# Loading a in blocks and turning it on VectorE and GpSimd instead of TensorE, in a fused RWKV-7 and gated-cosine kernel

## The chip, the cores and the metric

The kernel runs on one core of one Trainium2 chip. The metric is device time in microseconds of one execution, as the median of several runs. TensorE is called PE in the profile (its weight loads PEld), VectorE DVE, ScalarE ACT, GpSimd POOL, and SyncE, which issues most transfers, SP.

## What is computed

Two blocks follow each other: a recurrent attention (RWKV-7) over 768 steps for 4 batches x 8 heads with head size 40, and then a feed-forward layer on its output, 3072 tokens x 320 features, with 2048 hidden features.

```python
for t in range(S):
    kt, vt, rt = (k[:, :, t], v[:, :, t], r[:, :, t])
    wt, at, bt = (w[:, :, t], a[:, :, t], b[:, :, t])
    y[:, :, t] = np.einsum('bhd,bhde->bhe', rt, state)
    Sa = np.einsum('bhde,bhe->bhd', state, at)
    state_decay = state * wt[:, :, None, :] - np.einsum('bhd,bhe->bhde', Sa, bt)
    state = state_decay + np.einsum('bhd,bhe->bhde', vt, kt)
...
h = x @ w_in          # x is y, as tokens x (heads * head size)
g = h * np.cos(h)
return g @ w_out
```

All data is float32 on the chip; the two weight matrices arrive as float64 words and are rounded to float32 by the kernel itself (the items `t`, `e`, `m`, `p` of the order, each written `c`).

## The kernel before

**Units.** The sequence is cut into chunks of 64 steps (C). A unit is one chunk of two batches: its 128 partitions are 2 batches x 64 steps, its free dimension 8 heads x 40 features, padded to 64 (DP). There are 24 units (NU), handled in pairs (u, u+1) at the start of their work and one by one after that. Units of the same parity carry the same two batches.

**Within a chunk** the recurrence becomes matrix products. W is the running product of w over the steps of the chunk. The matrices need the feature dimension on the partitions (64 partitions for each of two heads, four pairs of heads `j` side by side, and in each the two batches' 64 steps: a tile of [128, 4, 128]). The steps of a unit, by their names in the order:

- `Lw La Lb Lk Lv Lr`: the loads (`load`, L128 to L149). A unit's a is loaded by two transfers of 64 steps x 8 heads x 40 features, one for each batch, in rows of 160 bytes.
- `pw` (`p1_w`): four PE transposes of w for each unit. For units 0 to 3 a scan on DVE makes the running products; from unit 4 on w arrives from memory as running products already (made for four chunks at a time on the tile `ws` by `scan`, `wj`, `sd`, stored by `ws`), and ACT copies them out of PSUM into `wb`; POOL takes the last column (`wc`) and puts a one in front (`from_one`).
- `pa` (`p1_a`): a, turned and multiplied by W. From unit 4 on: two PSUM banks, four PE transposes into each (`turned`, L370), and one product on DVE for each unit, out of PSUM into `aT` (`a_W`, L422).
- `rw` (DVE, reciprocal of W, then b times it on POOL), `pb` (b turned on PE), `pn` (the 64 x 64 products of a and b, copied by ACT), `K` (k over W on POOL, and v beside it), `v`, `k` (turned), `g` (products of k with a and v with r).
- `inv` and its steps `i`: for four units at a time a triangular inverse on DVE, 32 x 32 blocks in each of 128 partitions, with block transposes on DVE (L539, L555, L564; L617 for the first four units); `H`, `R` and `F`, `S` put the blocks together on PE.
- `t`, `q`, `ag`, `xa`, `s`, `z`: the chain from unit to unit, which hands on the state (`qz`), and at its end the result `yt`, multiplied by W on POOL (L840, 128 x 512, as the new product of the change).
- `T`, `X`: the result goes to memory and comes back as the tokens' transposed input `xT` of the second block (units 0 and 1 go straight, `Y`).

**The second block** is cut into 12 groups of tokens (two units each) x 4 parts of the hidden features, and each of these into four pieces on PE, written `M`: two of the first matmul (`ph`, L75), and two of the second (`po`, L75), which belong to the part before. Between them stand the steps `r`: rounding and cosine on ACT and DVE (L922 to L933); in the last groups (G0 on) the second matmul uses seven products in place of eight, for which DVE and POOL form sums (L981 to L989) and POOL sums of the weights (`B`, L965 to L969). `o` stores a result from SP.

**Order.** Nothing is reordered by a scheduler: `tc.manual_schedule()` keeps the instructions of each engine in the order in which they are issued, and that order is the long string `PLAN`, written out by a search. A name in it issues the whole step on all its engines and queues. A `^` makes the next PSUM tile begin with one matmul of the identity, 128 x 256, whose result is overwritten: padding on PE (`busy`, L348). A name that begins with L or f and ends with `a` issues its transfers from ACT's queue, all others from SP's. Each engine and each queue works strictly in order, so a step that waits holds up whatever stands behind it there; SP has no notion of the pieces and runs ahead of PE until something makes it wait.

The tiles into which a is loaded are two, one for each parity (`nat_a0` and `nat_a1`; units 2 and 3 use a part of w_in's place), so the load of unit u waits until unit u - 2 has been read out of its tile. PSUM has a pool of four banks (`at`) for nearly all steps of the first block, two for `ph` and two for `po`.

Of the kernel before, what the change touches and what calls it, by code (L numbers as in the profile page):

```python
# [20 lines left out]
def kernel(  # L21
# [12 lines left out]
    nc = tc.nc  # L34
# [93 lines left out]
    def load(u, names, via=nc.sync, parts=range(NB)):  # L128
        t0 = C * (u // 2)
        for n in names:  # L130
            if n == "r" and u < 4:
                x = r[NB * (u % 2) : NB * (u % 2) + NB, :, t0 : t0 + C, :].rearrange("b h t d -> (b h) (t d)")
                to = pick(nat[n, u], 0, (1, C * H * D * NB // P))
                via.dma_start(to, x.rearrange("h (g n) -> h g n", g=P // H // NB))
                continue
            for i in parts:
                at_u = src[n][NB * (u % 2) + i, :, t0 : t0 + C, :]
                if n == "w" and u >= 4:
                    at_u = wd[u // 4][NB * (u % 2) + i].rearrange("h s t d -> h (s t) d")
                    at_u = at_u[:, t0 % P : t0 % P + C]  # L140
                to = nat[n, u][blk[i], :, :D]
                if n in "vr":
                    for f in range(2):
                        via.dma_start(
                            pick(nat[n, u][blk[i]], f * DP, (2 * DP, HH), (1, D)),
                            at_u[f * HH : (f + 1) * HH].rearrange("h t d -> t h d"),
                        )
                else:
                    via.dma_start(to, at_u.rearrange("h t d -> t h d"))  # L149
# [1084 lines left out]
    with tc.manual_schedule():  # L1234
# [51 lines left out]
        def inv_begin(q):  # L1286
# [13 lines left out]
            ^ z0 c z1 ^ ^ v2 Y0 Lw4 La4 c Lw5 c Lk2 K2 Y1 La5 rw4 c ^ S3 f8 M Lk3 c f13 f9a M c c c f10 rw5  # L1300
            k2 K3 r S2 Lk4 c r c r ^ ^ t2 c c r g2 r H1 c c r ^ ^ pw4 k3 c f11 Lw7 M c f12 c c M c c ag2 r r
            Lb7 c q2 Lr3 c c wf2 c M r c c xa2 r f14 R1 pa4 c r c Lb6 M pb4 c f15 r c scan2 s2 c c pn4 La6 M
            Lw6 c c z2 lo4 ^ M v3 rw6 c c f16 c r La7 ^ g3 c wj2 t3 ^ pw6 f17 T2 ag3 c c rw7 q3 c r r c c c
            M r xa3 f18 ^ pa6 c c c M c s3 Lr4 pb6 f19 r r sd2 z3 c c M M c c pn6 M X2 lo6 r Lv4 inv1 r T3
            Lb8 X3 r c c i i i i t4 r r i i ws2 i r i M ^ v4 K4 Lk5 k4 i ^ M i g4 Lv5 i i M r i i r Lr5 r i
            M r r i i K5 r i ^ ^ ag4 i i i q4 o i i i M M M v5 r Lw9 i Lw8 r r La9 xa4 r i i r M M La8 i i i
            i pw8 i r M i wf3 t5 k5 i inv2 pa8 g5 M Lr7 H2 r Lv6 r Lb9 rw8 r r Lv7 M Lb10 H3 R2 r M ag5
            scan3 r Lk6 rw9 q5 Lr6 xa5 s4 wj3 M Lb11 s5 z4 M pb8 r Lw10 Lw11 v6 o T4 r K6 z5 La10 r r pw10 M
            rw10 La11 k6 T5 v7 rw11 R3 X4 pn8 Lk7 X5 Lr9 pa10 M r lo8 r sd3 K7 pb10 g6 pn10 Lr8 Lk8 k7 ws3 i
            i i M i lo10 M r g7 i i t6 t7 Lv9 r La13 r i i r M Lb12 i M r ag6 i i i r q6 i M i ag7 xa6 M i i  # L1310
            q7 wf4 Lw13 M r r r r o Lb13 i i Lv8 s6 r i i xa7 M r z6 T6 s7 Lw12 M t8 i i i K8 M z7 r v8 i
            Lk9 M i k8 pw12 r g8 i r r o v9 M ag8 r q8 i r rw12 K9 i M xa8 T7 Lr10 M X6 Lb14 k9 M rw13 r i
            t9 i i Lv10 i i i r La12 X7 r pb12 g9 M inv3 scan4 H4 Lk10 H5 Lw15 v10 pa12 r wj4 Lw14 r La14 R4
            Lb15 pn12 lo12 r M sd4 s8 M r r r z8 Lr11 M r ag9 q9 K10 M rw15 o t10 La15 r T8 rw14 k10 xa9
            pw14 Lb16 Lv11 pb14 r g10 s9 M pa14 z9 pn14 o M R5 ws4 r M M i lo14 Lk11 i r Lv12 r r r Lw16 r i
            i Lw17 v11 ag10 Lr12 K11 La16 Lv13 Lk12 i M T9 q10 M k11 i i i r t11 i X8 M r i r i X9 r xa10
            g11 s10 M r r i i rw16 ag11 q11 i i M M r xa11 r i z10 La17 r s11 r M M r Lr13 v12 i K12 r T10 i
            i Lb17 t12 i k12 pw16 pa16 M rw17 X10 i Lr14 M Lk13 r r r r La19 g12 M M r r v13 i M M i i i i i
            i i i r z11 ag12 r M M r r r i Lv14 r q12 M M i i i H6 r T11 r H7 M Lw19 r r La18 M K13 r R6
            Lk14 R7 xa12 r M v14 k13 s12 X11 M r pb16 r Lb19 wf5 z12 r Lw18 r pn16 K14 Lb18 r M scan5 o Lv15  # L1320
            M lo16 t13 k14 o g13 r pw18 rw18 M Lb20 M rw19 ag13 q13 r r T12 M pa18 xa13 r r r pb18 Lk15 wj5
            inv4 X12 r M s13 M Lr15 sd5 M pn18 r r r lo18 z13 M i r i M o K15 v15 r La21 k15 r t15 i Lr16 i
            i Lv16 t14 g15 T13 g14 M ag14 q14 Lk16 M r r r X13 r i i i i M r r M xa14 ag15 M q15 M r i i
            Lr17 Lv17 o r r xa15 r r i r i M ws5 M Lw20 i i s15 s14 i M Lw21 i z15 z14 M r r rw20 r r r M M
            pw20 r v16 K16 i i Lk17 i M M T14 i o r r K17 i r v17 i r M M k17 i r La20 i i r i i M Lb21 t17
            t16 k16 T15 i i pa20 Lb22 g17 Lw22 M i r Lk18 r i r r o g16 X14 M M r i r Lv18 La23 ag16 rw21
            q16 M Lr19 M i X15 r xa16 r r Lb23 r H8 H9 pb20 M R8 r R9 M s16 r M z16 M r K18 ag17 Lw23 rw23 r
            q17 r rw22 Lr18 r La22 r M M Lv19 r xa17 pw22 pa22 k18 T16 o pb22 pn20 lo20 s17 M M v19 r r v18
            r M r r r M g18 inv5 X16 z17 Lk19 pn22 i lo22 T17 i i i M M o r K19 k19 M r r r r r M g19 M M
            t18 i i Lr21 i i X17 r i r r t19 Lv20 i i M Lr20 r r i Lv21 i i B1 M i ag18 i B0 r q18 M i i  # L1330
            ag19 xa18 M i r i r i r s18 r r M r i M i i q19 r r o r M xa19 z18 Lk20 K20 s19 M r r r r B3 T18
            i z19 Lk21 v21 B2 K21 r M r r i M B6 k20 r v20 r M M r g20 r r r X18 r k21 r o M r M t20 r r t21
            T19 M ag20 B7 q20 B5 M Lk22 r i B4 r i r g21 xa20 r r M X19 M i i ag21 r r q21 i r r i i M M i r
            r xa21 Lv22 M r r H10 r H11 M r r R10 Lr23 r R11 r M Lr22 s21 s20 M o r z20 r Lv23 K22 T20 X20 r
            r r r r o r z21 r M M M M v23 Lk23 v22 r r r M r T21 M t23 K23 X21 t22 r r r r k22 k23 r M g22
            g23 M ag22 q22 M r r M r r r r r r r M M r r r xa22 M M r r r r ag23 q23 r r M M xa23 r r r M r
            r r M s23 r o r r s22 M M r z22 T22 r z23 r r M r r M r r r M M M M T23 r r r r r r r r r X22
            X23 M M r r r r r o r r M M r r M M r r r ^ M r r o M r r r r M M r M r r r o r r M r r r M M M
            M r r r r r r r r M r M o o
# [75 lines left out]
```

## Time and profile before

| what | value |
|---|---|
| median of 3 runs | 758.38 us (757.45 to 758.88) |
| the profiled execution | 761.06 us, its span 759.1 us |
| granted TensorE clock | 0.994 of full speed |
| PE | 739.2 us busy, 97% |
| DVE | 549.9 us, 72% |
| ACT | 400.4 us, 53% |
| POOL | 228.9 us, 30% |
| chain that ended last | PE 82%, DVE 7%, ACT 4%, DMA 3% |
| SP's queue (q1) | 170,104 packets, 30.4% of 16 engines' span |

How to read it: the span runs from the first to the last instruction. A row of a group gives line, engine, operation and the tiles written and read, then how many there were and how long they took; a row in order of time begins with its start and its length in us, and may end with the idle time before it and what ended that. A float32 matmul appears as two instructions, a transpose as one; the length of a PE row contains latency that overlaps the next one's, so what PE is held by is the distance from one start to the next. SPq and ACTq are transfers being issued, not moved.

### The profile page before, as it was taken

The numbers are of one execution on the slowest core, as the hardware profiler recorded it, in microseconds if no ns is written. First come the engines' busy times: TensorE is split into PE (matmuls) and PEld (weight loads), VectorE is DVE, ScalarE is ACT, GpSimd is POOL, SyncE is SP. The second block draws the span as 40 slices with busy tenths as digits, with TensorE's granted clock in tenths as the row PEclk, the third lists the DMA queues.
The fourth block names the chain that finished last, engine by engine and source line by source line (L and its number), as shares of the span: only waits on it lengthen the run. The fifth ranks groups of instructions, "written<-read, shape, count | busy, mean of one in ns | idle before, by whom it ended". The sixth has DMA issues, their size and how long they took to land.

```text
span 759.1 us, 28518 instructions
## 1 busy us (share of the span) xinstructions
PE 739.2 (97%) x12360; PEld 604.4 (80%) x12360; DVE 549.9 (72%) x1133; ACT 400.4 (53%) x778; POOL 228.9 (30%) x400
## 2 busy tenths in 40 slices
PE   7999989999999999999999999999999999999997
PEld 6877867777887887888787877787877988898886
DVE  6798979999679896579737658755379885656554
ACT  1335577655576457545475644555654536444442
POOL 5304745501420343102213103123221744312111
PEclk9999999999999999999999999999999999999999
DMA  9463665344345224533133320541021311200100
GB/s 140 116 181 81 163 149 134 100 89 87 72 111 107 65 38 88 110 67 63 29 82 67 78 73 2 105 75 37 12 57 20 77 18 21 57 7 9 44 19 18
DMA packets 177796, 54.39 MB, mean 72 GB/s; under 512 B 152712, under 2 KB 173320, under 8 KB 177672
## 3 DMA queue, kind: packets, MB, share of 16 engines
q1 hardware_dynamic: 170104, 49.17, 30.4%
q10 hardware_dynamic: 7568, 3.41, 2.0%
q8 instruction: 97, 1.59, 0.9%
q14 instruction: 27, 0.22, 0.1%
HBM read 41.68 MB, written 10.81 MB: 69 GB/s over the span
## 4 chain that ended last, share of the span: by engine, by line
PE 82%; DVE 7%; ACT 4%; DMA 3%; issue 2%; SPq 1%; POOL 0%; ACTq 0%; DVEq 0%; POOLq 0%
PE ph L75 26%; PE po L75 23%; PE x0ps L75 5%; PE dps L75 4%; PE beside L75 3%; PE gram L75 3%; PE sps L75 3%; PE vT L370 2%; PE nps L75 2%; PE below L75 1%; PE qps L75 1%; PE aps L370 1%; PE wT L370 1%; PE seventh L75 1%; PE kT L370 1%
## 5 line engine op out<-in xcount | busy, mean ns | idle before, releaser
L75 PE MATMUL ph<-xT,w_in_sb 128*128 128x256 f32 x768 | 182.7, 386 | 1.0 <-DVE gT L933 0.7
L75 PEld LDWEIGHTS ph<-xT,w_in_sb 128*128 128x128 f32 x768 | 140.4, 190 | 28.8 <-issue 9.8
L75 PE MATMUL po<-w_out_sb,gT 128*128 128x320 f32 x512 | 147.9, 438 | 0.0
L922 ACT ACTIVATE turns<-ph,rnd 128x512 f32<-128x512 f32 x96 | 62.7, 685 | 146.2 <-PE ph L75 143.8
L75 PEld LDWEIGHTS po<-w_out_sb,gT 128*128 128x128 f32 x512 | 93.9, 190 | 35.8 <-issue 0.3
L926 DVE SCALAR_TENSOR_TENSOR turns<-turns,ph 128x512 f32<-128x512 f32 x96 | 63.9, 682 | 69.1 <-ACT turns L922 65.7
L933 DVE TENSOR_TENSOR gT<-ph,turns 128x512 f32<-128x512 f32 x96 | 64.9, 682 | 25.5 <-ACT turns L930 25.0
L825 POOL TENSOR_TENSOR qz<-qz,wc 128x160 f32<-128x160 f32 x44 | 20.8, 478 | 174.4 <-DVE qz L824 172.7
L930 ACT ACTIVATE turns<-turns,half_pi 128x512 f32<-128x512 f32 x96 | 69.3, 722 | 3.1
L929 ACT ACTIVATE turns<-turns 128x512 f32<-128x512 f32 x96 | 60.3, 628 | 10.0 <-DVE turns L926 9.8
L551 DVE TENSOR_TENSOR inv<-inv,inv_tmp 128x31 f32<-128x31 f32 (+15 forms) x155 | 59.9, 387 | 5.3
L547 DVE TENSOR_TENSOR inv_tmp<-u,inv 128x31 f32<-128x31 f32 (+15 forms) x155 | 57.6, 372 | 3.4
L75 PE MATMUL ph<-xT,w_in_tail 64*64 64x256 f32 (+1 forms) x672 | 52.0, 384 | 0.0
L982 POOL TENSOR_TENSOR bn<-gT 128x128 f32<-128x128 f32 x32 | 19.3, 604 | 102.0 <-DVE gT L933 95.3
L416 DVE RECIPROCAL rw<-nat_w 128x320 f32<-128x320 f32 x20 | 42.6, 2138 | 1.1 <-DMA nat_w<-wd 1.1
L417 POOL TENSOR_TENSOR bn<-nat_b,rw 128x320 f32<-128x320 f32 x22 | 20.2, 916 | 74.9 <-DVE rw L416 50.5
L75 PEld LDWEIGHTS ph<-xT,w_in_tail 64*64 64x64 f32 (+1 forms) x672 | 27.2, 140 | 14.3 <-issue 9.3
L792 DVE TENSOR_TENSOR sm<-sps,su 128x256 f32<-128x256 f32 x48 | 18.1, 417 | 22.0 <-PE sps L75 19.2
L840 POOL TENSOR_TENSOR yt<-yt,wb 128x512 f32<-128x512 f32 x24 | 30.8, 1284 | 5.8 <-DVE yt L835 5.7
L738 ACT COPY qz<-qps 128x256 f32<-128x256 f32 x44 | 14.2, 374 | 34.3 <-PE qps L75 34.2
L786 ACT COPY sm<-sps 128x160 f32<-128x160 f32 x48 | 13.6, 292 | 29.4 <-PE sps L75 16.3
L670 POOL TENSOR_TENSOR kn<-nat_k,rw 128x320 f32<-128x320 f32 x24 | 22.8, 949 | 16.9 <-DMA nat_k<-in_k_dram 16.8
(218 smaller groups left out, 1413.8 us busy)
## 6 DMA issues: line engine op xcount, KB each, us to landing
nat_k<-in_k_dram SPq DMA_DIRECT2D x48, 80.0 KB
out_dram<-ot SPq DMA_DIRECT2D x46, 80.0 KB
vp<-in_v_dram SPq DMA_DIRECT2D x88, 40.0 KB
xd<-yt SPq DMA_DIRECT2D x44, 80.0 KB
nat_a<-in_a_dram SPq DMA_DIRECT2D x43, 80.0 KB
nat_b<-in_b_dram SPq DMA_DIRECT2D x43, 80.0 KB
ws<-in_w_dram SPq DMA_DIRECT2D x5, 640.0 KB
wd<-ws SPq DMA_DIRECT2D x5, 640.0 KB
```

Of the source, the lines that this page charges most:

```text
L75: nc.tensor.matmul(o, lhsT=lhsT, rhs=rhs, start=start, stop=stop, skip_group_check=True)
L370: nc.tensor.transpose(ps[:, i * P : (i + 1) * P], x[:, 2 * i : 2 * i + 2].rearrange("p e d -> p (e d)"), ident)
L416: nc.vector.reciprocal(rw, wn)
L547: nc.vector.tensor_tensor(tmp, u[:, j : j + 1, :j].to_broadcast([P, Q - j, j]), x[:, j:, j : j + 1].to_broadcast([P, Q - j, j]), ALU.mult,)
L551: nc.vector.tensor_tensor(x[:, j:, :j], x[:, j:, :j], tmp, ALU.subtract)
L670: nc.gpsimd.tensor_tensor(unpad(kn_b[u % 2]), nat["k", u], G["rw", u], ALU.mult)
L840: nc.gpsimd.tensor_tensor(yt.rearrange("p j b t -> p (j b) t"), yt.rearrange("p j b t -> p (j b) t"), wx, ALU.mult)
L922: nc.scalar.activation(n, u, ACTF.Identity, bias=rnd, scale=1.0)
L926: nc.vector.scalar_tensor_tensor(ns[e], ns[e], -ROUND, us[e], ALU.add, ALU.subtract)
L929: nc.scalar.activation(n, n, ACTF.Abs)
L930: nc.scalar.activation(n, n, ACTF.Sin, bias=half_pi, scale=-2.0 * math.pi)
L933: nc.vector.tensor_tensor(gT[:, 2 * e : 2 * e + 2].rearrange("p f t -> p (f t)"), us[e], ns[e], ALU.mult)
```

## The change

From unit 4 on, a is loaded differently. The 128 partitions of the tile become four quarters of 32: two for the even heads and two for the odd heads, and of these one for features 0 to 31 and one for features 32 to 39. Within a quarter the 32 partitions are steps. Each half of a chunk (32 steps) has its own 64-column half, so one transfer carries 32 steps x 8 (batch, pair of heads) x 32 or 8 features: eight transfers for each unit, in rows of 128 or 32 bytes. With this layout, transposing every block of 32 x 32 on its own gives what the whole 128 x 128 transpose gave: features on the partitions. DVE does that with one instruction for each unit, from the tile straight into `aT`, whose parts it writes in runs of 64; POOL multiplies `aT` by W in place. The PE transposes of a and the DVE product out of PSUM, with the two PSUM banks of the step, are gone for units 4 to 23. Units 0 to 3 stay as they were.

The order string is a new one from the search. It has 96 `^` in place of 90, and the same steps otherwise; the loads of units 0 to 3, of k0 and k1 and of the first weights have partly changed between SP's and ACT's queue (`La2a`, `Lw3a`, `f0a`, `f1a` lose their `a`, `Lk0`, `Lk1` gain one), and many loads stand elsewhere against the pieces.

```diff
             if n == "r" and u < 4:
...
                 via.dma_start(to, x.rearrange("h (g n) -> h g n", g=P // H // NB))
                 continue
+            if n == "a" and u >= 4:
+
+                x = a[NB * (u % 2) : NB * (u % 2) + NB].rearrange("b (j e) t d -> e t (b j) d", e=2)
+                for m in range(2):
+                    for q in range(4):
+                        d = slice(Q * (q % 2), min(Q * (q % 2) + Q, D))
+                        via.dma_start(
+                            pick(nat[n, u][quad[q]], Q * m, (2 * Q, H), (1, d.stop - d.start)),
+                            x[q // 2, t0 + Q * m : t0 + Q * m + Q, :, d],
+                        )
+                continue
             for i in parts:
...
     def p1_a(u):
         if u >= 4:
-            ps = at("aps")
             for i in range(2):
-                turned(ps[i], nat["a", u + i])
-            for i in range(2):
-                a_W(u + i, ps[i])
+                aT = ring.tile([P, 4, P], F32, tag="aT", name="aT")
+                nc.vector.transpose(
+                    pick(aT, 0, (C, NB), (P, HH), (1, C)),
+                    nat["a", u + i].rearrange("p (b j) t -> p b j t", b=NB),
+                )
+                x = aT.rearrange("p j (b t) -> p (j b) t", b=NB)
+                nc.gpsimd.tensor_tensor(x, x, G["wx", u + i], ALU.mult)
+                G["aT", u + i] = aT
             return
...
         PLAN = """
-            ^ ^ ^ ^ ^ ^ pw0 La1 Lb1 Lw2 Lk0 La3 La2a Lb3 Lw3a ^ ^ ^ ^ pa0 ^ ^ ^ ^ ^ ^ ^ ^ pw2 Lb2 pb0 wf1
...
+            La1 Lk0a Lb1 Lw2 Lw3 La2 ^ ^ ^ ^ ^ ^ ^ ^ pw0 Lb2 La3 ^ ^ ^ pa0 ^ ^ ^ ^ ^ pw2 wf1 Lb3 ^ pb0 f2
...
+            Lw19 r r M pw18 pn16 T12 rw19 M K14 lo16 La19 pa18 M r r ag13 r q13 M Lv15 sd5 M r o r rw18 R7 r
...
+            Lw23 r r r Lk18 r r q17 K18 M Lb23 M rw23 xa17 pw22 k18 pb22 pn20 s17 lo20 o M M v19 La22 v18
+            pa22 r r M r M r Lk19 pn22 r r inv5 z17 M M r K19 r i lo22 g18 i i M i r M r r k19 Lr20 r t18 i
...
         """
```

More of the change, by code (lines that the diff above doesn't have):

```diff
@@ L1300 @@
[L1300 to L1314, printed above, removed]
@@ new lines @@
+            Lv0a Lr0a pa2 ^ ^ ^ ^ ^ ^ pn0 scan1 pb2 inv0 f0 pn2 i f3 i i i lo0 i i i i i i i i i K0 i i i
+            wj1 Lb5 lo2 Lb4 Lr1 Lk1a f1 ^ ^ ^ ^ ^ ^ v0 f4 ^ k0 ^ ^ g0 i ^ ^ ^ ^ ^ ag0 Lv1a f5a i c ^ ^ F0 K1
+            c ^ ^ ^ S0 ^ ^ k1 sd1 c f6 c c F1 c ^ v1 S1 xa0 c c c La4 c ^ ^ g1 ^ F3 c H0 c c Lr2 c ^ ^ ag1 c
+            xa1 Lv2 ^ ^ R0 c c ^ ^ ^ ^ F2 ws1 Lk2 c c c c c Lv3 ^ ^ s0 s1 c z0 v2 Lw5 c f7 Lw4 La5 K2 c z1 c
+            f8 rw5 ^ Y0 c Lk3 Lr3 S2 ^ Y1 ^ pw4 c M c c f9a rw4 ^ S3 c c c M c c r Lb6 ^ ^ k2 r c f10 r r c
@@ new lines @@
+            ag7 xa6 i M i q7 Lr8 i i i r M r i r s6 xa7 La13 wf4 r o Lb13 r M Lw13 r s7 i z6 v8 i M K8 i i M
+            r z7 r rw12 Lk9 k8 M r t8 t9 r g8 r K9 Lr9 i Lr10 pw12 M ag8 r i i i i T6 Lv10 q8 M T7 M i i i i
+            xa8 i rw13 r M r v9 k9 H4 r H5 g9 M pa12 r X6 r R4 Lw15 pb12 Lb14 s8 X7 La15 v10 scan4 r pn12 o
+            z8 M M r r lo12 Lk10 Lw14 Lb15 R5 La14 M K10 r ag9 rw15 q9 r M rw14 pw14 wj4 r xa9 k10 pb14 r
+            pa14 inv3 g10 Lr12 s9 M z9 pn14 M Lk11 M r i r r i i Lv11 r Lv12 r K11 i sd4 i r M t10 Lr11 i
@@ new lines @@
+            t11 M i i i ag10 lo14 i i i i q10 T8 M i r xa10 v11 r k11 M r ws4 i g11 r X8 s10 i r r M ag11 i
+            i Lw16 i i q11 M M z10 Lw17 Lk12 r r xa11 Lb17 M K12 r r o T9 i o M X9 r r v12 i k12 rw17 Lr13 M
+            M s11 r i r r Lk13 i Lv13 g12 M r r M i t12 r pw16 i T10 Lb16 rw16 i i v13 M i i M r z11 o r
+            La16 r Lw18 Lb18 o r ag12 i M La17 M wf5 r r T11 q12 X10 M Lb19 M i i K13 i xa12 r Lk14 r r H6
+            pa16 r M Lv14 M H7 R6 r X11 La18 inv4 r k13 M g13 Lr15 scan5 s12 M r r z12 r M wj5 t13 pb16 r
@@ new lines @@
+            Lv21 i B5 xa18 M i M r s18 i r r r M M q19 r Lv20 r r r r M xa19 B1 v20 i i v21 z18 K20 s19 M
+            Lr22 r T18 X18 r r z19 r r r k20 B4 o M r M g20 T19 B3 i i r r i Lk21 M K21 M ag20 i t21 r r r
+            t20 Lv23 r r r i i r r r i M M X19 k21 M i q20 i M r i Lr23 i B7 Lv22 r g21 xa20 r r M M r r B6
+            i r Lk22 r ag21 q21 i i r M M r r r r xa21 H10 o M M H11 R10 r r r r r M s21 s20 M r z20 r r r r
+            r r z21 r M M r M M r r r r r K22 Lk23 K23 v23 r v22 M r r r M t22 R11 k22 k23 M T20 g22 g23 M r
@@ L1340 @@
+            r o X20 M M r r r r r ag22 q22 r T21 r X21 M M r r r r r r r o xa22 t23 M r M ag23 q23 r M M
+            xa23 M r r o r M r r s22 r r s23 r r M M r r z22 z23 M M r T22 T23 X22 r r r r r r M X23 M M r M
+            r r r r r r r r M M o r r r r M r r M o o r r r M M r r r r r r r r r M M M M r r r r r r r M M
+            r r M M r M M r r r r r r r r M M o o
         """
```

46 lines of the change are left out of this document (17 added, 29 removed).

## The prediction

> **What bounds the kernel now.** I read the page's busy table first, then the stretches of time (busy us of each engine and its share of instructions), because an average over 759 us hides stages.
>
> ```profile
> span 759.1 us, 28518 instructions
> PE 739.2 (97%) x12360; PEld 604.4 (80%) x12360; DVE 549.9 (72%) x1133; ACT 400.4 (53%) x778; POOL 228.9 (30%) x400
> ...
> 0.00:84.00 84.00, 77.28 (x1579) 64.34 (x1580) 67.83 (x130) 31.10 (x66) 35.46 (x78) 0.96 0.64 130
> 84.00:200.00 116.00, 109.80 (x1860) 86.38 (x1859) 104.67 (x206) 74.71 (x140) 44.23 (x65) 1.00 0.47 112
> 253.00:700.00 447.00, 446.71 (x7581) 364.75 (x7583) 306.75 (x638) 240.59 (x470) 125.37 (x222) 1.00 0.26 53
> 700.00:759.00 59.00, 52.80 (x338) 46.04 (x330) 30.55 (x73) 22.02 (x35) 11.69 (x18) 0.98 0.10 27
> ```
>
> From 253 to 700 us PE (the first busy column) idles 0.3 us, while DVE (the third) has 140 us to spare: there a matmul less is time less. (From 700 us on, PE's 6 us of idleness are the last products and the last store, which the change leaves alone.) Up to 200 us it is otherwise. Part of PE's busy time is padding (the `^` of the order, two matmuls of 128x256 each), and DVE is 90% busy from 84 to 200 us: there DVE and the transfers set the pace. So I cost the change in two parts, early and late.
>
> Then PE and its rows in order of time (start, us, line, what), at the start and in the late part:
>
> ```profile
> 10.93 3.62 PE L75 MATMUL wT<-ident 128*128 128x256 f32 x16
> 14.39 0.60 PE L370 MATMUL wT<-ident,w_in_sb 128*128 128x128 f32 x4
> 18.18 0.66 PE L370 MATMUL wT<-ident,w_in_sb 128*128 128x128 f32 x4 [3.19 <-DMA w_in_sb<-in_w_dram]
> 109.79 0.66 PE L370 MATMUL aps<-ident,nat_a 128*128 128x128 f32 x4 [1.52 <-ACT x L768]
> ...
> 528.32 1.04 PE L370 MATMUL aps<-ident,nat_a 128*128 128x128 f32 x8
> 529.20 0.60 PE L370 MATMUL kT<-ident,kn 128*128 128x128 f32 x4
> 529.63 1.04 PE L370 MATMUL bT<-ident,bn 128*128 128x128 f32 x8
> 530.60 1.16 PE L75 MATMUL nps<-aT,bT 40*64 40x64 f32 x64
> ```
>
> The eight transposes of a pair of units hold PE from 528.32 to 529.20, 0.88 us (each row's length counts the last one's latency too, so I take start to start). At the start PE stands 3.19 us for unit 3's w.
>
> Last, rows that price the new work (ns min/median/max):
>
> ```profile
> L422 DVE TENSOR_TENSOR aT<-aps,wb x24: 627/681/692, 11.9 to 529.8; 128x512 f32<-128x512 f32 x24
> L539 DVE STREAM_TRANSPOSE u<-nt x6: 1245/1246/1246, 32.3 to 549.6; 128x1024 f32<-128x1024 f32 x6
> L617 DVE STREAM_TRANSPOSE w_in_sb<-rt x4: 445/445/445, 54.5 to 90.2; 128x256 f32<-128x256 f32 x4
> L564 DVE STREAM_TRANSPOSE rn<-inv x5: 2071/2110/2168, 182.3 to 621.9; 128x1024 f32<-128x1024 f32 x5
> L840 POOL TENSOR_TENSOR yt<-yt,wb x24: 1264/1276/1448, 75.9 to 701.3; 128x512 f32<-128x512 f32 x24
> L551 DVE TENSOR_TENSOR inv<-inv,inv_tmp x155: 191/377/975, 151.9 to 621.7; 128x31 f32<-128x31 f32 x10, 128x60 f32<-128x60 f32 x10, 128x87 f32<-128x87 f32 x10, 128x112 f32<-128x112 f32 x10
> L149 SPq DMA_DIRECT2D nat_a<-in_a_dram x43: 595/633/1288, 2.5 to 507.7; - x43
> ```
>
> **Part by part.** The profiled execution took 761.06 us (span 759.1 and 2.0 around it), 2.7 above the median of 758.38. I work out differences from its rows and take them from the median.
>
> PE loses 80 transposes, ten pairs of units at 0.88 us: 8.8 us. Six pairs (units 12 to 23) stand after 253 us: -5.3 us there in full. Four (units 4 to 11) stand before about 200 us: 3.5 us under DVE's cover.
>
> The order changes PE's tile shape more often: 137 round trips between full 128-row matmuls and smaller ones against 133, counted in the two instruction orders. The bT row holds PE 0.97 us where eight transposes followed by their like hold it 0.88: 0.09 us a change, 0.18 a round trip, +0.7 us, charged to the late part. Late part: -4.6 us.
>
> DVE loses 20 products of 0.681 us and gains 20 transposes of 128x512, of which the trace has none. Bounds: half of L539 (0.62) and half of L564, whose input is strided (1.06). The new one reads a straight run and writes runs of 64, like L539 and L617; a line through these two gives 0.71, which I take. DVE: 20 x (0.71 - 0.68) = +0.6 us (-1.2 to +7.5). In the late part DVE's 140 us of idle time cover it; without that cover the upper end counts.
>
> POOL gains 20 products like L840, 20 x 1.28 = 25.5 us, on an engine 30% busy. Each waits for DVE's transpose, with kn, wc, bn and the state product qz queued behind it on POOL; DVE's transpose waits for the load, with the steps of the piece at work queued behind it. From landing to both products of a pair takes about 0.7 + 2 x 1.28 = 3.3 us; the matmuls that want them (`pn`) follow at least two pieces or some 30 transposes and small products later, more than 4 us of PE. Cost 0; up to 2 us each at the tightest pairs.
>
> SP: a unit's a is issued by 8 DMAs, not 2. At 0.63 us, about 0.66 from one to the next, that is 5.3 us for 1.3, 120 issues or 79 us more on SP's queue. Behind them stand the other loads and the stores of yt. The order has moved loads into slacker places: up to the first piece 88 issues of per-unit transfers for 60, between pieces 64 and 72 42 for 8, but 123 for 116 between pieces 24 and 48 (179 to 286 us), SP's fullest stretch. I take 0; the dear end is a rival. Packets: 1024 more a unit; a packet of SP's queue took on average 30.4% of 16 x 759.1 us over 170,104, 22 ns, so at most 1.4 us a unit over 16 engines that are a third busy: 0.
>
> The start: unit 3's w is no longer the last thing on ACT's queue (there behind ACT's copies), but on SP right after unit 2's. PE's wait of 3.19 us for it goes, and with it the later start of everything behind (wn, the reciprocals, `pn2`, the inverse that fills DVE from 32 us). Its next limit is unit 3's b, issued behind the 640 KB of ws; that is needed some 5 us after w. Of padding, 11 `^` fewer stand before the fifth piece, 18 more between there and the 41st and one fewer later (net +6, at 2 x 0.216 us each, from the x16 row): the order expects PE to reach its pieces earlier and to wait more afterwards, as it must where DVE sets the pace. Also the two PSUM banks of aps go, and waits like the 1.52 us at 109.79. The early part is bounded by 0 (DVE's work up to 200 us is the same) and by 3.2 + 3.5 = 6.7 us (start and transposes both in full). DVE idles 11 us between 84 and 200, so some can be pressed out: I take half, -3.5.
>
> Sum: -4.6 - 3.5 = -8.1: 750.3 us.
>
> **The rivals.**
> (1) The early part gains nothing: DVE, with the same work, ends it where it did, and the new `^` fill what PE saved. For: DVE 90% busy, more padding. Against: 3.19 us of pure waiting go at the very start of the chain. 758.4 - 4.6 = 753.8.
> (2) Slower: SP. Units 19 and 22 are loaded with no piece (22: one v) between load and transpose, and the start has 28 more issues (18 us) on SP before the first piece. If the extra 4.0 us of issue come out on PE in full at four units, +16: 766. It decides from 8.1 us in all. Against: 556 DMAs at about 0.64 us fill 354 of SP's 759 us, and it runs ahead of PE unless a store holds it.
> (3) POOL's products hold DVE. L551, two SBUF inputs, is 0.377 in the median and 0.975 at worst, while L539, one input, is 1.245 to 1.246 in all six. At the 0.6 us that the worst L551 loses, the eight early products cost DVE 4.8 us, which eats the early gain: 758.4 - 4.6 - 3.5 + 4.8 = 755.1. If each held DVE for its whole 1.28 us, 10.2 us: 760.5, slower; it decides from 8.1 us, that is 1.0 us a product.
>
> [...]
>
> **How the numbers follow.** No change can be told from one of 0.2%, 1.5 us. Forecast 0.48 (its own range 746 to 752.5), (1) 0.26, (2) 0.17, (3) 0.09. Of (2) a mild form with 8 us lost lands within 0.2%: 0.04. The rest of it, 0.13, and the strong form of (3), 0.05, make slower 0.18; the mild form of (3), 0.04, is still faster, so faster is 0.48 + 0.26 + 0.04 = 0.78. The range goes from 745 (the early gain in full, and waits for PSUM gone) to 761, which takes in (1) and (3).
>
> **What would show it.** PE has 80 fewer L370 rows and stays over 99% busy from 250 to 700 us; the first ph matmul starts some 3 us before 83.7; no 3 us wait for unit 3's w; the new transposes near 0.71 us; POOL near 255 us; SP near 430 us of issues. Wrong if DVE waits for nat_a (above all units 19 and 22) or PE's nps for POOL add up to over 8 us, or the first part ends later than 200 us.

## The result, and the profile after

The changed kernel takes 764.43 us (763.63 to 766.19, 4 runs) against 758.63 for the kernel before on the same chip: a ratio of 1.0082, interval 1.0063 to 1.01. That is 5.8 us slower where 8.1 us faster were forecast. On a second chip the same kernel came out at 1.0044 (1.002 to 1.0068; experiment e5). Single executions of one kernel spread widely, 758.55 to 767.43 us among the 12 of e5, and the spread goes with the granted clock (0.993 to 0.995 in the four fastest of them, 0.989 in the slowest). So below the medians are compared through the kernel before on the same chip, and the profiles, one execution of each kernel, stretch by stretch.

The page of the kernel after, its busy table and two lines of it:

```profile
span 764.5 us, 28556 instructions
...
PE 743.0 (97%) x12292; PEld 601.9 (79%) x12292; DVE 552.1 (72%) x1133; ACT 400.8 (52%) x778; POOL 255.6 (33%) x420
...
q8 instruction: 97, 1.59, 0.9%
...
L447 POOL TENSOR_TENSOR aT<-aT,wb 128x512 f32<-128x512 f32 x20 | 26.9, 1366 | 11.2 <-DVE aT L442 11.1
```

The parts did what they were said to do. PE has 68 matmuls fewer, 80 transposes less and 12 more of padding (six `^`). POOL is at 255.6 us, DVE 2.2 us higher. In the stretches of time (the first busy column is PE, the third DVE) the late part has not become shorter:

```profile
0.00:84.00 84.00, 75.30 (x1553) 61.35 (x1554) 64.93 (x129) 29.96 (x65) 34.38 (x77) 0.92 0.67 130
84.00:200.00 116.00, 112.47 (x1718) 86.72 (x1717) 104.96 (x196) 71.83 (x134) 48.09 (x62) 1.00 0.49 113
253.00:700.00 447.00, 443.93 (x7517) 361.13 (x7516) 307.70 (x639) 241.26 (x471) 142.43 (x236) 1.00 0.28 56
700.00:764.00 64.00, 58.45 (x476) 50.76 (x474) 34.39 (x83) 24.47 (x39) 12.33 (x19) 0.99 0.09 25
```

For 253 to 700 us PE now idles 3.1 us where it idled 0.3, and in the first 84 us the granted clock is 0.92 for 0.96. PE's rows in order of time (start, us, tile, count, and in brackets the idle time before the row and what ended it) show where:

```profile
1.71 6.73 PE L75 MATMUL wT<-ident 128*128 128x256 f32 x16 [1.71 <-POOL ident masks.py:199]
14.96 1.04 PE L381 MATMUL wT<-ident,w_in_sb 128*128 128x128 f32 x8
...
23.42 1.37 PE L75 MATMUL nps<-aT,bT 40*32 40x64 f32 x116
26.57 0.33 PE L75 MATMUL nps<-aT,bT 40*32 40x64 f32 x12 [1.79 <-issue]
...
30.80 4.99 PE L75 MATMUL vT<-ident 128*128 128x256 f32 x12
...
59.24 1.81 PE L75 MATMUL beside<-w_in_sb,rt 32*32 32x32 f32 x59 [1.57 <-issue]
...
189.88 1.56 PE L75 MATMUL sT<-ident 128*128 128x256 f32 x6
215.17 1.13 PE L75 MATMUL nps<-ident 128*128 128x256 f32 x4
225.33 0.70 PE L75 MATMUL bT<-ident 128*128 128x256 f32 x2
...
285.75 0.38 PE L75 MATMUL gram<-aT,kT 40*64 40x64 f32 x9 [0.76 <-issue]
...
295.85 0.31 PE L75 MATMUL dps<-vvm,kn 64*64 64x104 f32 x3 [0.70 <-issue]
```

The wait of 3.19 us for unit 3's w is gone: its transposes are part of the x8 row at 14.96. In its place stand waits that nothing in the profile ends ("issue"): 6.6 us in all on PE for 1.1 before, 4.4 us of them in the opening. Each of them lies in the middle of a run of small products. Behind the first comes a stretch at half clock (granted clock 0.50 from 28.4 to 35.1 us; 12 matmuls of padding at 30.80 take 4.99 us). And padding stands at 189 to 226 us, where before had none.

To compare, I cut both profiles at the same work: at the first piece and at piece 22 (counted from 0), with which the third part of the second group of tokens begins. Windows of before, then of after:

```profile
0.00:83.70 83.70, 76.98 (x1578) 64.07 (x1578) 67.71 (x129) 31.10 (x66) 35.16 (x77) 0.96 0.64 130
83.70:179.10 95.40, 89.80 (x1407) 70.38 (x1404) 85.09 (x174) 63.69 (x120) 34.87 (x47) 1.00 0.53 128
179.10:759.10 580.00, 572.46 (x9379) 469.94 (x9378) 397.09 (x831) 305.63 (x593) 158.91 (x277) 1.00 0.26 54
```

```profile
0.00:84.40 84.40, 75.65 (x1554) 61.46 (x1554) 65.29 (x130) 30.36 (x66) 34.78 (x77) 0.92 0.67 131
84.40:184.30 99.90, 96.44 (x1402) 73.85 (x1403) 89.75 (x172) 63.60 (x119) 42.52 (x51) 1.00 0.54 125
184.30:764.50 580.20, 570.87 (x9336) 466.54 (x9336) 397.08 (x833) 306.85 (x596) 178.26 (x293) 1.00 0.27 53
```

So in this pair of profiles the opening lost 0.7 us, the middle 4.5, and the late part, from which 4.6 us were to come, 0.2. In the middle DVE is busy 4.66 us longer and idles as long as before (10.3 and 10.2 us), so its longer work fits the loss; but PE, with its padding, is fuller still there (96.44 of 99.9 us), and e3 below gives back 1.9 of the 4.5 us by taking the padding away. 2.4 us of that DVE work stood ahead of the first piece before (67.71 for 65.29).

### The profile page after: what moved, and what is told of

Read it like the earlier page. It is cut to its first block, busy times and chain, and to the rows that moved or that the text cites. A ratio compares the mean times of both kernels' runs of the same rounds, so it can differ in the third digit from the quotient of the medians.

```text
span 764.5 us, 28556 instructions
## 1 busy us (share of the span) xinstructions
PE 743.0 (97%) x12292; PEld 601.9 (79%) x12292; DVE 552.1 (72%) x1133; ACT 400.8 (52%) x778; POOL 255.6 (33%) x420
## 3 DMA queue, kind: packets, MB, share of 16 engines
q8 instruction: 97, 1.59, 0.9%
## 4 chain that ended last, share of the span: by engine, by line
PE 83%; DVE 8%; ACT 4%; issue 2%; DMA 2%; POOL 1%; SPq 0%; DVEq 0%; ACTq 0%; POOLq 0%
PE ph L75 27%; PE po L75 23%; PE x0ps L75 5%; PE dps L75 4%; PE gram L75 3%; PE beside L75 3%; PE vT L381 3%; PE nps L75 2%; PE sps L75 2%; PE qps L75 1%; PE kT L381 1%; PE below L75 1%; PE sT L737 1%; PE seventh L75 1%; PE bT L381 1%
## 5 line engine op out<-in xcount | busy, mean ns | idle before, releaser
L566 DVE TENSOR_TENSOR inv<-inv,inv_tmp 128x31 f32<-128x31 f32 (+15 forms) x155 | 59.9, 387 | 5.3
L75 PE MATMUL ph<-xT,w_in_tail 64*64 64x256 f32 (+1 forms) x672 | 53.7, 387 | 0.0
L721 DVE TENSOR_TENSOR ag<-gram,su 128x256 f32<-128x256 f32 x48 | 18.0, 416 | 22.1 <-PE gram L75 22.0
L447 POOL TENSOR_TENSOR aT<-aT,wb 128x512 f32<-128x512 f32 x20 | 26.9, 1366 | 11.2 <-DVE aT L442 11.1
L784 DVE COPY x<-x0ps 128x416 f32<-128x416 f32 x24 | 14.0, 585 | 20.7 <-PE x0ps L75 20.6
```

The source lines that it names most:

```text
L75: nc.tensor.matmul(o, lhsT=lhsT, rhs=rhs, start=start, stop=stop, skip_group_check=True)
L447: nc.gpsimd.tensor_tensor(x, x, G["wx", u + i], ALU.mult)
L566: nc.vector.tensor_tensor(x[:, j:, :j], x[:, j:, :j], tmp, ALU.subtract)
```

## Experiments

Theory A: the new order costs, by its padding and by what it does to the opening. Theory B: the new path of a costs, by its eight DMAs, by GpSimd and by waits it brings. All 16 runs with what each gave; the last three columns are from the rows in order of time of the profiled execution (us to the first piece, from there to piece 22, from there to the end). In each group of four, "before" ran on the same chip (760.64, 759.76, 758.98 and 759.61 us).

| kernel | median | ratio to before (interval) | to first piece | to piece 22 | to end |
|---|---|---|---|---|---|
| before | | | 83.7 | 95.4 | 580.0 |
| after | 764.43 | 1.0082 (1.0063, 1.01) | 84.4 | 99.9 | 580.2 |
| e1 old order, new path | 778.39 | 1.0231 (1.0201, 1.0262) | 83.2 | 104.3 | 589.9 |
| e2 new order, old path | 774.04 | 1.0173 (1.0146, 1.02) | 84.0 | 104.2 | 584.7 |
| e3 after, no late padding | 756.93 | 0.994 (0.9917, 0.9963) | 80.6 | 98.0 | 575.0 |
| e4 after, opening padding 6 | 763.86 | 1.004 (1.0017, 1.0063) | 79.2 | 99.4 | 579.1 |
| e5 after again | 763.86 | 1.0044 (1.002, 1.0068) | 81.2 | 99.6 | 578.6 |
| e6 before, no late padding | 759.65 | 1.0007 (0.9988, 1.0026) | 81.0 | 95.3 | 580.2 |
| e7 after, early 29 gone | 760.52 | 1.0008 (0.9983, 1.0033) | 83.4 | 98.8 | 577.0 |
| e8 as e3, f2 later | 754.87 | 0.9944 (0.9918, 0.997) | 78.8 | 99.2 | 575.0 |
| e9 old order, product on DVE | 779.79 | 1.0257 (1.0228, 1.0286) | 82.2 | 103.5 | 588.9 |
| e10 before, a in 8 DMAs | 779.84 | 1.0267 (1.0231, 1.0304) | 82.4 | 106.6 | 591.2 |
| e11 as e8, product twice | 772.95 | 1.0171 (1.0149, 1.0193) | 80.4 | 104.5 | 583.3 |
| e12 as e8, opening padding 6 | 754.5 | 0.995 (0.9931, 0.9968) | 81.8 | 98.9 | 575.3 |
| e13 new order, old path, 8 DMAs | 772.89 | 1.0173 (1.0136, 1.0209) | 78.9 | 103.0 | 584.5 |
| e14 as e8, product on DVE | 758.08 | 0.9987 (0.997, 1.0004) | 79.7 | 99.8 | 576.4 |
| e15 after, late six gone | 763.92 | 1.0051 (1.0029, 1.0074) | 78.9 | 99.8 | 578.9 |
| e16 after, f2 later | 762.6 | 1.0031 (1.0013, 1.005) | 81.7 | 99.5 | 580.0 |

### Order or path (e1, e2)

e1 is the changed kernel with the order string of before; e2 is the kernel before with the new string.

```diff
         PLAN = """
-            La1 Lk0a Lb1 Lw2 Lw3 La2 ^ ^ ^ ^ ^ ^ ^ ^ pw0 Lb2 La3 ^ ^ ^ pa0 ^ ^ ^ ^ ^ pw2 wf1 Lb3 ^ pb0 f2
...
+            ^ ^ ^ ^ ^ ^ pw0 La1 Lb1 Lw2 Lk0 La3 La2a Lb3 Lw3a ^ ^ ^ ^ pa0 ^ ^ ^ ^ ^ ^ ^ ^ pw2 Lb2 pb0 wf1
...
         """
```

> The order of before, with the new path of a (small loads, VectorE's transposes, GpSimd's products). Theory A (the new order costs: its padding before pieces 2 to 31 and its longer opening): the path keeps its late gain of 4.6 us, so 752 to 756 us. Theory B (the path costs: 8 small DMAs a unit, instruction rows of PE that wait for 'issue', GpSimd against VectorE): the loss stays, 762 to 768 us.

> The new order, with a loaded, turned and multiplied as before. Theory A: the order's loss stays and the path's gain goes, 766 to 772 us. Theory B: without the path there is no loss, 755 to 760 us.

Neither theory is right for both. The new path in the old order costs 18 us (so B), and the new order with the old path costs 13 us (so A); together they cost 3 to 6. In the new order the path is worth what the transposes promised: from the first piece on, 688.9 us with the old path against 680.1 and 678.2 with the new one, 8.8 to 10.7 us for the 8.8 of 80 transposes. The loss of the change lies in the order; but the old order cannot carry the path.

### What the path breaks in the old order (e9, e10, e13)

e9 moves e1's product to VectorE. e10 leaves the old path and order alone and only splits a's loads as finely as the new path does; e13 is the same split in the new order.

```diff
-                nc.gpsimd.tensor_tensor(x, x, G["wx", u + i], ALU.mult)
+                nc.vector.tensor_tensor(x, x, G["wx", u + i], ALU.mult)
```

```diff
+                elif n == "a" and u >= 4:
+                    for m in range(2):
+                        for d in (slice(0, Q), slice(Q, D)):
+                            via.dma_start(
+                                nat[n, u][P // 2 * i + Q * m : P // 2 * i + Q * m + Q, :, d],
+                                at_u[:, Q * m : Q * m + Q, d].rearrange("h t d -> t h d"),
+                            )
                 else:
                     via.dma_start(to, at_u.rearrange("h t d -> t h d"))
```

> The order of before with the new path of a (1.023 of before), and the product by W^T on VectorE instead of GpSimd. Theory 'GpSimd's queue is what the new path breaks in the old order' (the product waits on GpSimd for a's load and turn, with kn behind it; PE stood 3.1 us for kn and 3.3 us for aT): most of the 18 us come back behind piece 22, 755 to 765 us, in spite of 0.68 us more of VectorE a unit. Rival 'the loads come too late, whoever multiplies': it stays at 772 us or more, with the waits put down to VectorE or the load.

> The kernel before with the loads of a from unit 4 on split into 8 DMAs of 32 steps by 32 (or 8) columns, as many and as large as in the new path, into the old layout, all else unchanged. Theory SP (120 more issues, 79 us, come out on PE where a store or load stands behind them): 764 to 778 us. Rival 'SP has slack for them': 758 to 762 us, and the loss of the old order with the new path lies in the turn and the product.

> The new order with the old path of a (1.017 of before), and the loads of a from unit 4 on in 8 DMAs of 32 steps by 32 (or 8) columns. Theory 'the new order has made room on SP's queue': no change, 1.015 to 1.020 of before, against 20 us for the same split in the old order. Rival 'the split costs in any order': 1.025 or more.

GpSimd is not it: e9 stays at 779.79. The split alone is: e10 costs 20 us with everything else as before. Its rows in order of time, on SP's queue, DVE and PE:

```profile
89.60 0.43 DVE L275 TENSOR_SCALAR w_out_sb<-words 128x512 int32<-128x512 int32 x1 [6.27 <-DMA words<-in_moe_w_out_dram]
...
120.58 3.99 SPq L151 DMA_DIRECT2D nat_a<-in_a_dram  x8
124.61 1.27 SPq L156 DMA_DIRECT2D nat_w<-wd  x2
...
129.97 2.15 DVE L423 RECIPROCAL rw<-nat_w 128x320 f32<-128x320 f32 x1 [5.42 <-DMA nat_w<-wd]
...
136.23 1.11 PE L377 MATMUL wT<-ident,nat_w 128*128 128x128 f32 x4 [5.09 <-ACT s L732]
```

What comes late is not a, but what stands behind it on SP's queue: eight issues of a take 3.99 us, w is issued only then, and DVE waits 5.42 us for it and PE 5.09 a little later; at 89.60 DVE waits 6.27 us for weights of the second block (in before 1.50 at most in this stretch). In the new order the same split costs nothing that can be measured (e13 1.0173, e2 1.0173). So rival (2), SP, has the right mechanism, and its 16 us come near the 20 here by luck, as they were worked out for the new order: the old one has not made room for the split, the new one has.

### Padding (e3, e6, e7, e15)

e3 drops every `^` behind the first piece from the changed kernel, e7 only the 29 up to piece 14, e15 only the six between pieces 23 and 30; e6 drops the 13 that the kernel before has behind its first piece. Two places of e3:

```diff
-            f8 rw5 ^ Y0 c Lk3 Lr3 S2 ^ Y1 ^ pw4 c M c c f9a rw4 ^ S3 c c c M c c r Lb6 ^ ^ k2 r c f10 r r c
+            f8 rw5 ^ Y0 c Lk3 Lr3 S2 ^ Y1 ^ pw4 c M c c f9a rw4 S3 c c c M c c r Lb6 k2 r c f10 r r c
...
-            r i xa4 La9 r i pw8 r M v5 ^ ^ M i i i i i i i Lv7 ^ t5 r g5 H2 rw8 M rw9 r H3 Lr7 Lb10 R2 pa8 M
+            r i xa4 La9 r i pw8 r M v5 M i i i i i i i Lv7 t5 r g5 H2 rw8 M rw9 r H3 Lr7 Lb10 R2 pa8 M
```

> The changed kernel without the 33 padding steps behind the first piece. Theory A in its form 'padding itself is on the path': these 33 took 14.7 us of PE's time behind the first piece against 5.5 before the change; up to 10 us come back, 755 to 760 us. Theory A in its form 'the steps come too early, padding only fills their waits': the waits return as idle time, 763 to 766 us. Theory B: 762 to 766 us, padding is not the cause.

(There are 35 steps, not 33; from start to start they take 17.2 us.)

> The kernel before without its 13 padding steps behind the first piece. If padding behind the first piece costs what it takes of PE whatever the order: 13 x 0.43 = 5.6 us less, 0.993 of before. If the few of before stood in waits for VectorE, which come back as idle time: 0.998 to 1.001, and only the new order's placing of padding is dear.

> The changed kernel without the 29 padding steps between pieces 1 and 14, with its six between pieces 23 and 30 kept. Theory 'the dear ones are the six late ones' (PE is the bound there: 2.6 us of padding in whole, and the shifted blocks of instructions): 0.5 to 2.5 us less than the changed kernel, 1.005 of before. Theory 'the early 29 are dear': 5 to 7 us less, 0.999 to 1.001 of before.

> The changed kernel without its six padding steps between pieces 23 and 30, where PE is the bound. They take 2.8 us there by the rows; 2 to 4 us less than the changed kernel, the same stretch (piece 22 to 38) 71.6 us for 73.7; 1.001 to 1.004 of before. If they only fill a wait: 0 to 1 us.

Padding is where the loss went: without it the changed kernel is faster than before, 0.994 for 1.0044 (e5), some 8 us. It isn't dear as such: in the order of before its removal changes nothing (1.0007), the time comes back as idle time. And the steps do not add up: the 29 alone are worth 3.3 us, the six alone nothing that can be measured, both together about 8. The windows of e3 and the table show why:

```profile
0.00:80.60 80.60, 72.00 (x1554) 58.64 (x1554) 65.52 (x130) 30.66 (x66) 34.76 (x77) 0.96 0.73 136
80.60:178.60 98.00, 88.63 (x1345) 66.89 (x1345) 89.33 (x172) 63.00 (x118) 42.50 (x51) 0.95 0.55 128
178.60:753.60 575.00, 567.12 (x9324) 464.01 (x9324) 397.43 (x833) 306.95 (x596) 178.71 (x293) 1.00 0.27 54
```

From piece 22 on it takes 575.0 us, 5.0 less than before: the forecast late gain. In the middle 7.8 us of PE's work (96.44 to 88.63) go, yet only 1.9 us of time: DVE's 89.33 us of work stay, and PE's granted clock falls to 0.95. The six sit where PE is the bound: in the stretch from piece 22 to 38 e15 and e3 take 71.6 us for the 73.7 of the changed kernel and e7. But e15 gives that back in waits of PE, its rows in order of time:

```profile
278.11 0.68 PE L75 MATMUL gram<-rT,vT 40*64 40x64 f32 x29 [0.61 <-issue]
288.83 0.81 PE L75 MATMUL dps<-sm,bn 64*40 64x104 f32 x25 [1.27 <-issue]
503.56 0.87 PE L381 MATMUL bT<-ident,bn 128*128 128x128 f32 x6 [0.49 <-issue]
529.91 3.72 PE L75 MATMUL ph<-xT,w_in_sb 128*128 128x256 f32 x16 [0.77 <-issue]
```

These are 3.1 us, where the changed kernel had 2.0 behind piece 22; e3 and e7 have none of them. (A wait of 0.3 us near 710 us stands in all of them, and in before.) Behind piece 38, where none of these kernels has padding, this is the difference: 506.5 us in the changed kernel (505.0 in e5), 507.3 in e15, 503.3 in e3 and in e7. So the waits go when the 29 go, and stay when the six go; the 2.1 us that the six hold up are kept only where the 29 are gone too.

### The waits for "issue" (e5, e8, e16)

> The changed kernel itself, beside the next three on one chip: 1.006 to 1.010 of before. In its profile PE should again wait without a releaser ('issue') near 26, 51, 59, 286, 296 and 510 us, at the same instructions (a block of some 254 PE instructions apart), if those waits are PE waiting for its own instructions; at other instructions if they are chance.

They come at the same instructions. I counted PE's weight loads and matmuls from the start up to each wait of 0.3 us or more:

| kernel | opening | late |
|---|---|---|
| after | 436, 690, 1453, 1962 | 9814, 10317, 17395 |
| e5 after again | 436, 1453, 1962 | 9814 (10317: 0.2 us) |
| e16 after, f2 later | 690, 1706 | 9814, 10317 (17395: 0.3 us) |
| e15 after, late six gone | 436, 690 | 9815, 10318, 17396, 18408 |
| e3 after, no late padding | 436, 690, 1453, 1962 | none |
| before | 1961 | none |

The counts lie whole numbers of steps of 251 to 255 apart (690 - 436 = 254, 1453 - 690 = 3 x 254.3, 10317 - 9814 = 2 x 251.5; a few records are missing), and they stay while the tiles change: six `^` less ahead of them (e15) put other matmuls at the same late counts, and the waits are there. The queue named instruction in the page moved 97 packets and 1.59 MB, 16.4 KB each, and PE's 24,584 instructions are 253 to a packet. In the trace's transfers the first such packet starts at 23.7 us and takes 1.5 us; PE goes on at 26.57, 1.3 us after its end, and at the other waits of the opening 1.3 to 1.5 us after the end of a packet. So I take these waits to be PE's for its next block of instructions. The first of them stands where the block before it was used up fast: 116 products with their weight loads in 1.4 us. One such wait costs 0.2 to 2.0 us here.

What makes it late in the opening is tested by e8 (on e3) and e16 (on the changed kernel), which move one step:

```diff
-            La1 Lk0a Lb1 Lw2 Lw3 La2 ^ ^ ^ ^ ^ ^ ^ ^ pw0 Lb2 La3 ^ ^ ^ pa0 ^ ^ ^ ^ ^ pw2 wf1 Lb3 ^ pb0 f2
+            La1 Lk0a Lb1 Lw2 Lw3 La2 ^ ^ ^ ^ ^ ^ ^ ^ pw0 Lb2 La3 ^ ^ ^ pa0 ^ ^ ^ ^ ^ pw2 wf1 Lb3 ^ pb0
-            Lv0a Lr0a pa2 ^ ^ ^ ^ ^ ^ pn0 scan1 pb2 inv0 f0 pn2 i f3 i i i lo0 i i i i i i i i i K0 i i i
+            Lv0a Lr0a pa2 ^ ^ ^ ^ ^ ^ pn0 scan1 pb2 inv0 f0 pn2 i f3 i i i lo0 f2 i i i i i i i i i K0 i i i
```

> The changed kernel without the 35 padding steps behind the first piece (its earlier run: 0.994 of before), and with f2 (two DMAs of 256 KB of the experts' weights, issued at 17 us) put behind lo0. Theory 'PE's wait near 25 us is for its instructions, held up by these DMAs': the wait of 1.25 to 1.8 us at the 436th instruction goes, as does the half clock behind it, and the first piece starts 2 to 4 us earlier; in the total 0 to 3 us, 0.990 to 0.994. Rival 'the wait is not the DMAs': it stays, 0.994.

> The changed kernel with f2 behind lo0 and nothing else: the two DMAs of 256 KB leave the time in which PE wants its 436th instruction. Theory 'the opening's share is the wait for instructions and the half clock after it': the first piece at 79 to 81 us for 81 to 84, and 1.5 to 3 us less than the changed kernel, 1.002 to 1.004 of before. Rival 'VectorE sets the pace up to piece 22 anyway': 0 to 1 us less, 1.004 to 1.007.

From 20 to 24 us the 16 DMA engines are full in the changed kernel (share 1.13; 0.24 in before), because f2's half megabyte is issued at 17 us; in e8 the share is 0.35. With f2 later the wait at the 436th instruction is gone in both, and over all profiles of the new order it is 0.7 to 2.0 us in the eight that have f2 early and under 0.2 us in the five that have it late. e8's rows:

```profile
22.32 1.47 PE L75 MATMUL nps<-aT,bT 40*32 40x64 f32 x128
...
26.70 0.41 PE L75 MATMUL nps<-aT,bT 40*32 40x32 f32 x21 [0.34 <-issue]
27.05 2.86 PE L75 MATMUL vT<-ident 128*128 128x256 f32 x12
...
39.07 1.07 PE L75 MATMUL x0ps<-vvm,ag 64*64 64x104 f32 x32 [2.27 <-DVE vvm L725]
```

The twelve matmuls of padding take 2.86 us there for 4.99: the half clock behind the wait went with it. But another stretch at half clock, as long, begins at 39.75 us (four matmuls of padding at 40.07 take 2.07 us, 1.13 at 42.86 in the profile of e15), behind the next wait: PE stands 2.27 us for DVE's vvm. The theory holds for the wait, and its price fails: the total moves by 1 us or less (e16 1.0031 for e5's 1.0044, intervals that overlap; e8 0.9944 for e3's 0.994).

### The opening's padding (e4, e12)

```diff
-            La1 Lk0a Lb1 Lw2 Lw3 La2 ^ ^ ^ ^ ^ ^ ^ ^ pw0 Lb2 La3 ^ ^ ^ pa0 ^ ^ ^ ^ ^ pw2 wf1 Lb3 ^ pb0 f2
+            La1 Lk0a Lb1 Lw2 Lw3 La2 ^ ^ ^ ^ ^ ^ pw0 Lb2 La3 ^ ^ ^ pa0 ^ ^ ^ ^ ^ pw2 wf1 Lb3 ^ pb0 f2
```

> The changed kernel with 6 padding steps, not 8, ahead of its first transposes of w. If the later first transposes (8.3 us for 6.4) push the opening: the first piece starts 1 to 2 us earlier, and the whole takes 762 to 763.5 us. If the opening has slack, or is limited by loads: 764 to 765 us.

> The new order without padding behind the first piece, f2 later, and 6 padding steps, not 8, ahead of the first transposes of w. If PE's start sets the pace of the opening: the first piece 1.5 to 2 us earlier, 753 to 754 us, 0.992 of before. If the opening waits for its loads: 754.5 to 755.5 us.

e4 (1.004) cannot be told from the changed kernel (1.0044 to 1.0082), nor e12 (0.995) from e8 (0.9944), though the first transposes start 2.3 us earlier in e4 and 1.0 in e12. PE's start does not set the pace.

### GpSimd against VectorE (e11, e14)

```diff
                 nc.gpsimd.tensor_tensor(x, x, G["wx", u + i], ALU.mult)
+                nc.gpsimd.tensor_tensor(x, x, G["wx", u + i], ALU.mult)
```

> The new order without padding behind the first piece and f2 later (0.994 of before), and each of GpSimd's 20 products by W^T done twice, so that a is multiplied by W^T a second time. Theory 'GpSimd's products hold VectorE' (VectorE was 4.6 us longer busy with them than with the same order and the old path): VectorE's busy time rises by 3 to 6 us, and the stretch up to piece 22 by 1 to 2.5 us (8 of 20 products, and VectorE the bound there); 756 to 758 us. Rival 'no hold, only the product's own length': 754.5 to 755.5 us, VectorE unchanged.

> The new order and path without padding behind the first piece and with f2 later (0.994 of before), the product by W^T on VectorE. VectorE gets 20 products of 0.68 us and loses the hold. If the hold is 0.5 us a product, as the doubled products say (VectorE 10.2 us more for 20): VectorE's busy time rises by 13.6 less 4 to 10, to 555 to 561 us, and the whole is within 2 us, 0.993 to 0.997 of before. If the hold costs more than the product itself: faster, 0.990. If there is next to no hold: VectorE at 565 us, and 3 to 5 us slower, 0.998 to 1.001.

The busy tables on the page, first e8, which both are made from, then e11, then e14:

```profile
PE 728.7 (97%) x12222; PEld 590.7 (78%) x12222; DVE 551.6 (73%) x1133; ACT 400.1 (53%) x778; POOL 257.0 (34%) x420
```

```profile
PE 732.9 (95%) x12222; PEld 592.4 (77%) x12222; DVE 561.8 (73%) x1133; ACT 400.2 (52%) x778; POOL 283.1 (37%) x440
```

```profile
PE 730.2 (97%) x12222; PEld 591.6 (78%) x12222; DVE 562.7 (74%) x1153; ACT 400.1 (53%) x778; POOL 230.2 (30%) x400
```

Twenty more products on POOL make DVE, with the same instructions, 10.2 us longer busy, 0.51 each. The first twenty cost it less. Moved to DVE (e14) they take 0.80 us each, not the 0.68 that I had expected:

```profile
L447 DVE TENSOR_TENSOR aT<-aT,wb 128x512 f32<-128x512 f32 x20 | 16.0, 798 | 2.3
```

The lengths of DVE's other instructions, products and transposes of a left out, add up to 582.8 us in e14 and 586.8 in e8: 4.0 us, or 0.20 each, had been lost to them. (Against e2, the old path in the same order, DVE's 552.1 is 4.6 us more, 0.23 each.) The loss sits in few instructions: in the changed kernel one step of the inverse (L566, 128x240, at 479.98 us) that ran beside such a product took 1.37 us, where the four like it took 0.41 to 0.61. The hold is real, and at 0.20 us a product cheaper for DVE than doing the product there, at 0.80. In the total e14 is at 0.9987 of before and e8 at 0.9944, 0.4% slower, with intervals that just touch. e14's DVE lies between the cases of half a microsecond and of next to no hold, its time in the range of the latter. The doubled product costs 17 to 18 us in all, some five times what I expected: there is the hold, and a longer way from load to `aT`, to which I can't put shares.

## Why the prediction was wrong

**The late part, -4.6: the mechanism was right, padding and waits for instructions were not counted.** From piece 22 to piece 158, first before, then after:

```profile
179.10:670.02 490.92, 489.68 (x8577) 397.56 (x8577) 349.63 (x717) 270.62 (x534) 142.40 (x252) 1.00 0.29 60
184.32:675.47 491.15, 487.90 (x8533) 394.06 (x8533) 351.05 (x722) 270.80 (x534) 162.98 (x269) 1.00 0.30 59
```

PE is busy 1.8 us less. Padding there rose from nothing to 3.0 us, from start to start, so PE's other work fell by 4.8, near the 4.6 forecast. But PE's idle time rose from 1.2 to 3.3 us, and just so much are the three waits for its instructions (2.0 us). The step that failed is "18 more [`^`] between there and the 41st" piece, which I left in the part under DVE's cover. Six of the 26 there stand at 189 to 226 us, where PE is 99% busy. The waits were no term of the sum at all; they hang on where the blocks of instructions fall, and go with the early 29 steps (e7), not with the six (e15). e3, without padding, has the gain: 5.0 us.

**The start, -3.5: failed.** The wait for unit 3's w did go, as forecast. It was not the last thing in the way. The opening holds a full DMA load, PE's instruction blocks and, behind both, DVE: in the two profiles PE's waits for instructions grew from 0.9 to 4.4 us, the stretches at half clock from two of 3.4 us to two of 6.8 each, and when e8 removes the worst of it, vvm on DVE is late next. How much is lost differs from one execution to the next. Seven profiles have this opening (after, e2, e3, e5, e7, e13, e15): the first piece starts at 78.9 us in the two without half clock, at 80.6 to 84.0 with 6.8 to 10.2 us of it, and at 83.4 and 84.4 with 13.7. The five with the old opening (before, e1, e6, e9, e10) have 3.4 to 6.8 us of half clock and start it at 81.0 to 83.7. So the gain was there in executions at full clock, and on average (81.6 for 82.5 us) little of it was left. That the half clock comes from the waits is likely but not shown: such a stretch began within 2 us of the end of the wait at the 436th instruction in the five profiles where that wait was 1.25 us or more, and in none of the three where it was 0.7 to 1.0. I had asked what is late next only of the loads ("its next limit is unit 3's b").

**The early part's bound by "0 (DVE's work up to 200 us is the same)": failed.** The bound below nothing was missing. Up to piece 22 DVE's busy time is 152.8 us before and 155.0 after, and 4.7 us more of it lie behind the first piece, where DVE is 90% busy. This fits the middle's 4.5 us, but does not prove it: with the same DVE work e3 takes 1.9 us less there, so at most 2.6 are DVE's. Of the 4.7 some 2.4 were moved there by the order; of the 2.2 by which the sum grew, e2 with the old path has 0.7 (153.5 in all), and 1.5 came with the path, which is rival (3) in its mild form. Taking "half" of a gain on a stretch that I had just called bound by DVE had no row behind it, and the new order's own padding was left out of it. Without padding, rival (1), "the early part gains nothing", is what happens: it gave 753.8, and e3 is 0.994 to 0.995 of 758.38, 754 to 755.

**POOL and SP at 0.** POOL's products: 0.20 to 0.23 us of DVE each, in part in an early stretch where that counts. SP's 120 issues: 0 is right in this order (e13), 20 us in the other (e10). I had looked for the dear end in the new order's crowded stretches, and it is not there.

**Small terms.** The transposes on DVE took 0.653 to 0.711 us, median 0.670, for the 0.71 taken, so DVE's bill for the exchange is nil. DVE waited 1.6 us for a, once. POOL's 255.6 us and SP's 415 us of issues are near the 255 and 430 given; an issue of a small part of a took 0.45 us in the median, not 0.63.

The sum: forecast -8.1, profile +5.4. Of the 13.5 between them 4.2 are the opening (if all of the early 3.5 is put there), 4.5 the middle, 4.8 the late part; the first of these is within what single executions of one opening differ by.

Left open: how the 17 to 18 us of the doubled product divide, and why the 29 and the six steps of padding together are worth more than twice what they are worth one by one. Behind piece 22 the waits for instructions account for it, as told above; the rest of the 8 us was not traced. Open too is the share of the clock: beside e5, at 0.992 on average, the kernel before ran at 0.996.

e3, e8 and e12 (0.994 to 0.995) beat both kernels; between them nothing can be told.

## What to carry to other kernels

Padding cost nothing here where its time came back as idle time (e6, 1.0007 without 13 steps), and some 8 us where the new order put it (e3, 35 steps): look at which stretch each step of it stands in, and try the kernel without it. When a wait is removed near the start, ask what of all kinds is late next, the other engines' work and the engine's own instructions too, and not only the next load. The split of a's transfers was paid by what stood behind them on SP's queue, 20 us in the old order (e10) and nothing that can be measured in the new one (e13), so such a split has to be tried with a new order too, and an order and a path have to be tried apart before either is blamed.

## What the runs showed of the hardware

By the counts, PE gets its instructions in blocks of about 254 (packets of 16.4 KB, 0.9 to 1.5 us each in the opening). Its waits for "issue", 0.2 to 2.0 us each, stood at the ends of such blocks: the first in the opening behind products that used a block up in about 1.4 us, while transfers filled the DMA engines (share 1.13 from 20 to 24 us). Six `^` less ahead of them (e15) put other products at the same counts, 9815 and 10318 for 9814 and 10317, and an edit moved 2 to 3 us of such waits in or out of a stretch that it didn't touch (behind piece 38: 2.0 us in the changed kernel, 3.1 in e15, none in e7).

The stretches at half clock in the opening (granted clock 0.50) were two of 3.41 us in before and two of 6.83 after; one of 10.24 us stood behind 92 us in e7, whose granted clock was 0.981 over its 759.3 us. What sets their lengths was not shown.

POOL's products of 128x512 (1.28 us in the median) cost DVE time in other instructions: on average 0.20 us a product (e8 against e14), 0.23 (the changed kernel against e2) and 0.51 (e11 against e8); the step of the inverse told above took 1.37 us, its like 0.41 to 0.61. How the two engines get into each other's way was not shown.
